# k for the later head groups: loaded as bf16 blocks by GpSimd's casting DMA and transposed by SyncE's DMA instead of by TensorE

## The chip, the core and the metric

The kernel runs on one core of one Trainium2 chip. The metric is the device time of the whole program in microseconds (us), the median of several runs.

## What is computed

Causal block attention, followed by a two-branch feed-forward layer that keeps the larger branch:

```python
# q, k, v: [8 batches, 8 heads, 576 rows, 64] float32
scores = q @ k.T / 8                       # per batch and head
scores = where(pos_i // 64 >= pos_j // 64, scores, -1e9)   # 64-row blocks
attn   = softmax(scores)
x      = (attn @ v), heads side by side    # [4608 tokens, 512]
h1, h2 = x @ w1, x @ w2                    # w1, w2: [512, 1024]
out    = maximum(h1, h2) @ w_out           # w_out: [1024, 512]
```

## The kernel before, in words

**Tiles.** Heads are handled in pairs (two heads of 64 side by side fill 128 partitions), and two pairs form a *group*: 16 groups of 4 heads, two groups to a batch. For a pair p the scores need `qT` and `kT`, bf16 tiles of 128 x 576 with the head dimension on the partitions. There are four slots of each (`kT_r[p % 4]`), so the slot that group g fills was last read by group g - 2.

**How k becomes kT.** `load_qk(g)` (L112, its DMA at L120) brings 576 KB of q and 576 KB of k of a group, as float32, through SyncE's DMA queue; each waits for a tiny GpSimd memset (L119) that holds it back to its place in the order. `cast` (L132) turns each into bf16 on GpSimd one iteration later. `transposes` (L352) does 18 transposes of 64 x 128 on TensorE into two PSUM tiles, and their contents are copied out (L360), one half by VectorE and one by ScalarE. `T_AT` says when: the even pair of group g carries the transposes of q of group g + 1, the odd pair those of k. `pad_keys` (L378) then makes on GpSimd a small zero-padded copy `kz` of the last key blocks of each pair.

**The order is written by hand.** The engines execute the instructions in the order in which the program emits them; no scheduler moves anything. The start up to group 2 is spelled out. From group 3 on, one loop over g runs (an *iteration*, one per group), with an even pair a = 2g and an odd pair b = 2g + 1:

1. `region(tile_0(a), tile_1(a))`: scores (L371), exponentials on ScalarE (L395), masks on GpSimd (L400);
2. per pair: `fill` with some units of the feed-forward part, then `av` of the pair two back (L479, its results normalised by VectorE into `xp`, L485 and L486), then the transposes of that half, then more scores; after the odd pair `pad_keys` of the next two pairs;
3. `pool_work`: GpSimd's loads of v (L136, casting DMAs of 64-element rows), the memsets that release the next loads, and the casts.

**The feed-forward part** is a list of units with a due time. `h_unit` (L215) multiplies x by w1 - w2 and `y_unit` (L257) makes a 128 x 512 piece of the output and stores it through SyncE's queue (L263). `fill(n)` runs some n matmuls of these wherever TensorE would otherwise wait. A unit may only start when the tokens that it needs are marked done (`done_tokens`).

**x by DMA.** From group 4 to 14 the attention output `xp` is turned into `xT` by two DMA transposes on SyncE's queue (`x_dma`, L497), issued after the odd pair's `av` in the iteration after the group's own. A batch is complete with its second group, so the second group's transposes must land before the first `h_unit` of that batch, which the loop starts after the first half-`fill` of the next iteration. The first `h_unit` reads the first group's two rows of `xT` (c = 0, 1), then, after six matmuls of `av`, the second group's (c = 2, 3).

**Semaphores of DMAs.** The DMAs of each kind rotate over eight semaphores, so that a DMA waits for the eighth before it on its kind of queue.

Of the kernel before, what the change touches and what calls it, by code (L numbers as in the profile page):

```python
# [9 lines left out]
BF16 = mybir.dt.bfloat16  # L10
# [4 lines left out]
def kernel(  # L15
# [10 lines left out]
    nc = tc.nc  # L26

    B, H, S, D = q.shape
    P = 128
    BLK = 64  # L30
# [14 lines left out]
    NG = NPAIR // 2  # L45
    GPB = HP // 2
# [36 lines left out]
    raw = ctx.enter_context(tc.tile_pool(name="raw", bufs=3))  # L83
# [10 lines left out]
    NV, NA, NT = 3, 4, 4  # L94
    qT_r = [ring.tile([P, S], BF16, name=f"qT{r}") for r in range(NT)]
    kz_r = [ring.tile([P, 3 * BLK], BF16, name=f"kz{r}") for r in range(NT)]
    kT_r = [ring.tile([P, S], BF16, name=f"kT{r}") for r in range(NT)]
# [12 lines left out]
    dve, pool, act = nc.vector.tensor_copy, nc.gpsimd.tensor_copy, nc.scalar.copy  # L110

    def load_qk(g, queues, gated=False):  # L112
        b, u = divmod(g, GPB)
        for nm, src, queue in (("q", q, queues[0]), ("k", k, queues[1])):
            if queue is None:
                continue
            raws[nm, g] = t = raw.tile([P, 2, RPP * D], FP32, name=f"{nm}raw")
            if gated:
                nc.gpsimd.memset(t[:, 0, :1], 0.0)  # L119
            queue.dma_start(  # L120
                out=t[:],
                in_=src[b, 4 * u:4 * u + 4].rearrange(
                    "(s h) (p t) d -> (h p) s (t d)", h=2, t=RPP),
            )

    def cast(nm, g, parts):
        t = raws[nm, g].rearrange("p s (t d) -> p t s d", d=D)
        if (nm, g) not in qk_n:
            qk_n[nm, g] = qkn.tile([P, RPP, 2, D], BF16, name=f"{nm}n")
        n = qk_n[nm, g]  # L130
        for copy, j0, j1 in parts:
            copy(out=n[:, j0:j1], in_=t[:, j0:j1])  # L132

    def load_v(b, c):
        rows = min(P, S - c * P)
        nc.gpsimd.dma_start(  # L136
            out=vv_r[b % NV][P - rows:, c, :, :D],
            in_=v[b, :, c * P:c * P + rows, :].rearrange("h p d -> p h d"),
        )
# [7 lines left out]
    for j in range(d_ff // WB):  # L147
        row, n = (1, j) if j < 3 else (3, 0)
# [22 lines left out]
    dve, pool, act = nc.vector.tensor_copy, nc.gpsimd.tensor_copy, nc.scalar.copy  # L171
# [174 lines left out]
    def transposes(nm, g, copies):  # L346
        n = qk_n.pop((nm, g))
        pts = [ps_m.tile([P, RPP, NP], BF16, name=f"ps_{nm}T", tag="m") for _ in range(2)]
        for j in range(RPP):
            for i in range(2):  # L350
                r = slice(i * NP, (i + 1) * NP)
                nc.tensor.transpose(  # L352
                    pts[i][:, j, :], n[r, j].rearrange("p s d -> p (s d)"), ident[r, r],
                )

        def copy_out(which=(0, 1), part=(0, NP), copy=None):
            p0, p1 = part
            for i in which:
                t = (qT_r if nm == "q" else kT_r)[(2 * g + i) % NT]
                (copy or copies[i])(  # L360
                    out=t[:, p0 * RPP:p1 * RPP].rearrange("q (p j) -> q p j", j=RPP),
                    in_=pts[i][:, :, p0:p1].rearrange("q j p -> q p j"),
                )
        return copy_out
# [67 lines left out]
    def tile_0(p):  # L432
        u = ps_s.tile([P, 2, 512], FP32, name="ps_s", tag="s")
        scores(p, u, 0, 0, 0, 512)
        return lambda: (exp(p, u, 512, 0), mask(p, 0))

    def tile_1(p):
        u = ps_s.tile([P, 2, 512], FP32, name="ps_s", tag="s")
        scores(p, u, 0, 0, 512, 64)
        scores(p, u, 64, 1, 128, 448)  # L440
        return lambda: (exp(p, u, 512, 512), mask(p, 576))

    def tile_2(p):
        u = ps_s.tile([P, 2, 512], FP32, name="ps_s", tag="s")
        corner_scores(p, u, 320)
        scores(p, u, 0, 2, 256, 320)
        scores(p, u, 384, 3, 448, P)

        def out():
            exp(p, u, 512, 1024)  # L450
            nc.scalar.activation(
                out=aT_r[p % NA][BLK:, :, 1536:AW], in_=u[BLK:, :, 320:320 + BLK],
                func=AF.Exp, scale=scale,
            )
            mask(p, 1024)
            mask(p, 1344)
        return out

    def region(*tiles):
        for out in tiles:  # L460
            out()
# [29 lines left out]
    def x_by_dma(g):  # L491
        return BY_DMA <= g < NG - 1

    def x_dma(g):
        b, u = divmod(g, GPB)
        for s in range(2):
            nc.sync.dma_start_transpose(  # L497
                out=xT[:, 2 * u + s, b * S:b * S + NCH * P].rearrange(
                    "p (t w) -> p t w", w=P),
                in_=xps[g][:, s].rearrange("p t a d -> p (t a d)"),  # L500
            )

    def x_out(g, t0=0, t1=NCH, copies=(dve, dve)):
        b, u = divmod(g, GPB)
        if x_by_dma(g):
            if u == GPB - 1:
                done_tokens[0] = (b + 1) * S
            return
        xp = xps[g]
        n = t1 - t0  # L510
        n_odd = min(t1, NCH - 1) - t0
        pe = ps_m.tile([P, 2, n, BLK], BF16, name="ps_xe", tag="m")
        po = ps_m.tile([P, 2, n_odd, BLK], BF16, name="ps_xo", tag="m")
        for s in range(2):
            for t in range(t0, t1):
                src = xp[:, s, t].rearrange("p a d -> p (a d)")
                nc.tensor.transpose(pe[:, s, t - t0, :], src[:BLK], ident[:BLK, :BLK])
                if t < NCH - 1:
                    nc.tensor.transpose(po[:, s, t - t0, :], src[BLK:], ident[BLK:, BLK:])
        dst = xT[:, 2 * u:2 * u + 2, b * S + t0 * P:b * S + t1 * P].rearrange(  # L520
            "p s (t h w) -> p s t h w", h=2, w=BLK)
        copies[0](out=dst[:, :, :, 0], in_=pe[:])
        copies[1](out=dst[:, :, :n_odd, 1], in_=po[:])
        if u == GPB - 1:
            done_tokens[0] = min(b * S + t1 * P, (b + 1) * S)
# [8 lines left out]
    def fill_of(g):  # L534
        if g == NG - 1:
            return 45
        left = 5 - g if g < 5 else 2 - (g - 5) % 2
        return -(-max(0, ready() - KEEP) // left)


    def pool_work(s):
        g, i = divmod(s, 2)
        if s == 4:
            load_qk(4, (SP, SP), gated=True)
        elif s == 5:
            load_qk(5, (SP, SP), gated=True)
            cast("q", 4, ((pool, 0, RPP),))
            cast("k", 4, ((pool, 0, RPP),))
        else:
            if i == 1 and g + 3 < NG:  # L550
                load_qk(g + 3, (SP, SP), gated=True)
            if i == 1 and g + 2 < NG:
                cast("q", g + 2, ((pool, 0, RPP),))
                cast("k", g + 2, ((pool, 0, RPP),))
            nb, j = divmod(s + 2, HP)
            if nb < B:
                for c in ((0, 1), (2, 3), (4,), ())[j]:
                    load_v(nb, c)

    T_AT = {s: [("qk"[s % 2], s // 2 + 1)] for s in range(NPAIR - 2)}  # L560
    T_AT[0] = T_AT[1] = T_AT[2] = T_AT[3] = []

    def t_pair(s):
        outs = [transposes(nm, g, (dve, act)) for nm, g in T_AT.get(s, [])]
        return lambda: [f() for f in outs]


# [3 lines left out]
    def av_with(p, n):  # L571
        av(p, [0, 1])
        fill(n)
        av(p, [2, 3, 4])
# [82 lines left out]
    outs = tile_0(4), tile_1(4)  # L657
# [13 lines left out]
    n = fill_of(GPB)  # L671
# [10 lines left out]
    for g in range(GPB + 1, NG):  # L682
        a, b = 2 * g, 2 * g + 1
        old = done_tokens[0]
        if x_due:
            x_out(x_due.pop())
        n, new = fill_of(g), done_tokens[0]
        region(tile_0(a), tile_1(a))
        lo, hi = max(3, n // 18), n * 2 // 9
        for p, tiles in ((a, lambda: (tile_2(a), tile_0(b))), (b, lambda: (tile_1(b), tile_2(b)))):  # L690
            if p == a and x_by_dma(g - 2):
                done_tokens[0] = old
            rest = fill(hi)
            done_tokens[0] = new
            fill(rest)
            av_with(p - LAG, lo)
            if p % 2 and x_by_dma(g - 1):
                x_dma(g - 1)
            copy_out = t_pair(p)
            outs = tiles()  # L700
            copy_out()
            region(*outs)
            if p % 2 and g + 1 < NG:
                pad_keys(p + 1)
                pad_keys(p + 2)
            pool_work(p)
        x_due.append(g - 1)
        fill(n - 2 * (lo + hi))
# [49 lines left out]
```

The softmax here doesn't subtract the row's maximum and nothing guards it: scores larger than these inputs give would overflow.

## Time and profile before

| What | Value |
|---|---|
| median of 3 runs | 259.0 us (258.83 to 259.49) |
| the profiled execution | 260.0 us, its span 258.2 us |
| instructions in the profile | 7195 |
| PE busy | 247.4 us, x2983 |
| VectorE, ScalarE, GpSimd busy | 136.1, 143.2, 110.4 us |
| TensorE clock granted | 1.00 throughout |
| one iteration of the loop, groups 5 to 13 | 13.0 us |
| DMA moved | 41.30 MB in 71265 packets |

The span is the time from the first to the last instruction of one profiled execution; 1.8 us of that execution lie around it. PE is TensorE's matmuls and PEld its weight loads, DVE is VectorE, ACT ScalarE, POOL GpSimd, SP SyncE. A matmul's recorded duration includes its way through the array, and matmuls overlap: the time that a block of them occupies is the distance between the starts of what comes before and after it.

### The profile page before, as it was taken

The page shows a single profiled execution, that of the slowest core. Times are in us where ns is not written, and L with a number is a line of the kernel's source. Part 1 is how long each engine was busy: PE and PEld are TensorE (multiplying, and loading weights), DVE is VectorE, ACT ScalarE, POOL GpSimd, SP SyncE. Part 2 cuts the span into 40 slices and gives each one's busy share as a digit, 9 for nine tenths or more (in the row PEclk, how much of TensorE's full clock was granted, in tenths as well). Part 3 has the DMA queues.
Part 4 walks back from the last instruction along what each step waited for, and adds up shares of the span by engine and source line. Part 5 has one row for each costly group of instructions (what it writes and reads, how often), then busy time and mean ns, then how long its engine had stood idle before and what let it go on. Part 6 is the DMA issues. An engine that isn't in the chain of part 4 may idle for free.

```text
span 258.2 us, 7195 instructions
## 1 busy us (share of the span) xinstructions
PE 247.4 (96%) x2983; PEld 139.1 (54%) x2983; DVE 136.1 (53%) x299; ACT 143.2 (55%) x200; POOL 110.4 (43%) x274
## 2 busy tenths in 40 slices
PE   7598899799999999999999999999999999999995
PEld 2346678646555555555555554546464655444444
DVE  4967986556584428451845184518550853443200
ACT  2798854476574857586757665766576431000111
POOL 1987950584637263726382638163813010000000
PEclk9999999999999999999999999999999999999999
DMA  6999999499569995998599949985977122202122
GB/s 244 316 206 307 217 251 246 156 102 253 129 162 257 144 188 135 245 154 225 114 244 143 186 145 224 168 196 141 91 109 110 44 56 80 83 0 81 43 104 99
DMA packets 71265, 41.30 MB, mean 160 GB/s; under 512 B 53568, under 2 KB 58048, under 8 KB 71232
## 3 DMA queue, kind: packets, MB, share of 16 engines
q1 hardware_dynamic: 28544, 31.27, 43.4%
q0 software_dynamic: 42272, 8.92, 39.9%
q10 hardware_dynamic: 416, 0.66, 0.7%
q8 instruction: 23, 0.38, 0.6%
q14 instruction: 10, 0.08, 0.1%
HBM read 34.60 MB, written 9.44 MB: 171 GB/s over the span
## 4 chain that ended last, share of the span: by engine, by line
PE 84%; DMA 8%; POOL 3%; ACT 2%; issue 1%; DVE 0%; SPq 0%; POOLq 0%; ACTq 0%
PE ps_y L257 36%; PE ps_h L215 22%; PE ps_o L479 10%; PE ps_s L371 8%; DMA qraw<-in_q_dram 5%; DMA kraw<-in_k_dram 3%; PE ps_qT L352 2%; PE ps_kT L352 2%; PE ps_w L341 1%; ACT aT L395 1%; PE ps_y L272 1%; PE ps_M L238 1%; POOL kn L132 1%; PE ps_s L389 1%; ACT qT L360 1%
## 5 line engine op out<-in xcount | busy, mean ns | idle before, releaser
L395 ACT ACTIVATE aT<-ps_s 128x1024 bf16<-128x1024 f32 (+2 forms) x100 | 95.8, 996 | 25.8 <-PE ps_s L371 24.2
L257 PE MATMUL ps_y<-wo_sb,g 128*128 128x512 bf16 x280 | 69.8, 379 | 0.0
L215 PE MATMUL ps_h<-xT,d_sb 128*128 128x512 bf16 (+3 forms) x320 | 69.2, 358 | 0.3 <-DVE d_sb L162 0.3
L220 DVE TENSOR_SCALAR g<-ps_h 128x512 bf16<-128x512 f32 (+3 forms) x80 | 50.7, 636 | 30.6 <-PE ps_h L215 28.8
L400 POOL MEMSET aT<- 64x128 bf16 x124 | 22.4, 200 | 81.8 <-ACT aT L395 81.2
L485 DVE RECIPROCAL rec<-ps_o 128x4 f32<-128x4 f32 (+1 forms) x64 | 12.1, 188 | 62.5 <-PE ps_o L479 61.7
L215 PEld LDWEIGHTS <-d_sb 128*128 128x128 bf16 x320 | 29.0, 98 | 29.1 <-issue 2.7
L479 PEld LDWEIGHTS <-aT 128*128 128x128 bf16 x960 | 37.2, 98 | 13.5 <-issue 0.8
L262 ACT COPY y<-ps_y 128x512 f32<-128x512 f32 x31 | 18.2, 587 | 44.5 <-PE ps_y L257 36.1
L257 PEld LDWEIGHTS <-g 128*128 128x128 bf16 x280 | 25.8, 98 | 29.8 <-issue 2.0
L479 PE MATMUL ps_o<-vv,aT 128*128 128x65 bf16 x960 | 39.8, 194 | 0.0
L257 PE MATMUL ps_y<-m_sb,xT 128*128 128x512 bf16 x140 | 38.2, 380 | 0.0
L136 POOL DMA_DIRECT2D vv<-in_v_dram x40 | 33.7, 848 | 1.6 <-issue 1.2
L371 PE MATMUL ps_s<-qT,kT 64*128 64x64 bf16 (+6 forms) x344 | 31.2, 280 | 1.6 <-ACT kT L360 0.7
L486 DVE TENSOR_TENSOR xp<-ps_o,rec 128x256 bf16<-128x256 f32 (+1 forms) x64 | 31.4, 491 | 2.2
L360 ACT COPY qT<-ps_qT 128x576 bf16<-128x576 bf16 (+1 forms) x17 | 10.3, 614 | 19.9 <-PE ps_qT L352 19.9
L132 POOL CAST qn<-qraw 128x1152 bf16<-128x1152 f32 (+1 forms) x16 | 16.9, 1058 | 9.1 <-DMA qraw<-in_q_dram 9.1
L257 PEld LDWEIGHTS <-xT 128*128 128x128 bf16 x140 | 12.2, 98 | 15.1 <-issue 3.5
L371 PEld LDWEIGHTS <-kT 64*128 64x128 bf16 x344 | 12.3, 94 | 11.0 <-issue 6.2
L132 POOL CAST kn<-kraw 128x1152 bf16<-128x1152 f32 (+1 forms) x15 | 17.1, 1140 | 1.4 <-DMA kraw<-in_k_dram 1.4
L360 ACT COPY kT<-ps_kT 128x576 bf16<-128x576 bf16 x15 | 9.6, 639 | 14.4 <-PE ps_kT L352 14.4
L207 POOL COPY g<-g 128x512 bf16<-128x512 bf16 x8 | 4.9, 614 | 20.7 <-DVE g L220 20.3
(58 smaller groups left out, 161.8 us busy)
## 6 DMA issues: line engine op xcount, KB each, us to landing
qraw<-in_q_dram SPq DMA_DIRECT2D x16, 576.0 KB, 5.0
out_dram<-y SPq DMA_DIRECT2D x35, 256.0 KB, 3.7
kraw<-in_k_dram SPq DMA_DIRECT2D x15, 576.0 KB, 5.8
vv<-in_v_dram POOLq DMA_DIRECT2D x32, 128.0 KB, 5.7
w1raw<-in_moe_w_dram POOLq DMA_DIRECT2D x4, 512.0 KB, 8.1
xT<-in_moe_w_dram POOLq DMA_DIRECT2D x4, 256.0 KB, 8.6
wo_sb<-in_moe_w_out_dram POOLq DMA_DIRECT2D x2, 512.0 KB, 10.0
kraw<-in_k_dram ACTq DMA_DIRECT2D x1, 576.0 KB, 5.6
```

The costliest lines, as they stand in the source:

```text
L132: copy(out=n[:, j0:j1], in_=t[:, j0:j1])
L136: nc.gpsimd.dma_start(out=vv_r[b % NV][P - rows:, c, :, :D], in_=v[b, :, c * P:c * P + rows, :].rearrange("h p d -> p h d"),)
L215: nc.tensor.matmul(pt[:, :w], d_sb[:, c, f * P:(f + 1) * P], xT[:, c, t0:t0 + w], start=(c == 0), stop=(c == NDM - 1),)
L220: nc.vector.tensor_scalar_max(g[:, f, m:m + w], pt[:, :w], 0.0)
L257: nc.tensor.matmul(py[:], lhs, rhs, start=(n == 0), stop=(n == len(terms) - 1),)
L262: (dve if i < 2 else act)(out=y[:], in_=py[:])
L360: (copy or copies[i])(out=t[:, p0 * RPP:p1 * RPP].rearrange("q (p j) -> q p j", j=RPP), in_=pts[i][:, :, p0:p1].rearrange("q j p -> q p j"),)
L371: nc.tensor.matmul(ps[:, hh, col:col + w], kT[r, k0:k0 + P], qT[r, q0:q0 + w], start=True, stop=True,)
L395: nc.scalar.activation(out=aT_r[p % NA][:, :, a0:a0 + w], in_=ps[:, :, :w], func=AF.Exp, scale=scale,)
L400: (eng or nc.gpsimd).memset(aT_r[p % NA][BLK:, :, a0:a0 + BLK], 0.0)
L479: nc.tensor.matmul(po[:, gi, hh, :], a[:, hh, a0:a0 + P], vv[:, c, h0 + 2 * hh, :], start=(mm == 0), stop=(mm == n_mm - 1),)
L486: nc.vector.tensor_mul(xp[:, :, ts[0]:ts[0] + n, p % 2].rearrange("q s t d -> q t s d"), po[:, :, :, :D], rec[:, :n].to_broadcast([P, n, 2 ...
```

## The change

From group 5 on, for k only:

- `load_qk` no longer loads k, and its memset, the cast on GpSimd, the 18 transposes on TensorE and the two copies out of PSUM are left out.
- `load_blocks` issues four casting DMAs from GpSimd's queue, one for each head of the group, in `pool_work` of the even pair of iteration g - 2, ahead of the v loads there. Each brings 9 blocks of 64 rows of 64 elements as bf16, into a tile that takes the place of the float32 one.
- `transpose_blocks` issues two DMA transposes on SyncE's queue, one per pair, after the even pair's `av` in iteration g - 1. Each reads 64 partitions x 9 x 128 elements and writes 128 partitions x 576 of `kT`.

Eleven groups (5 to 15) are concerned: 44 casting DMAs and 22 DMA transposes are added; 11 k loads, 11 memsets, 11 casts, 198 transposes on TensorE and 22 copies are removed. The rest of every engine's order is as before.

```diff
     def load_qk(g, queues, gated=False):
         b, u = divmod(g, GPB)
         for nm, src, queue in (("q", q, queues[0]), ("k", k, queues[1])):
-            if queue is None:
+            if queue is None or by_dma(nm, g):
                 continue
...
+    T_DMA = {nm: 5 for nm in "k"}
+    blk_n = {}
+
+    def by_dma(nm, g):
+        return g >= T_DMA.get(nm, NG)
+
+    def load_blocks(nm, g):
+        b, u = divmod(g, GPB)
+        blk_n[nm, g] = n = raw.tile([P, S // BLK, 2, D], BF16, name=f"{nm}b", tag=f"{nm}raw")
+        for h in range(2):
+            for s in range(2):
+                nc.gpsimd.dma_start(
+                    out=n[h * BLK:(h + 1) * BLK, :, s],
+                    in_=(q if nm == "q" else k)[b, 4 * u + 2 * s + h].rearrange(
+                        "(j p) d -> p j d", p=BLK),
+                )
+
+    def transpose_blocks(nm, g):
+        n = blk_n.pop((nm, g))
+        for h in range(2):
+            nc.sync.dma_start_transpose(
+                out=(qT_r if nm == "q" else kT_r)[(2 * g + h) % NT].rearrange(
+                    "q (j p) -> q j p", p=BLK),
+                in_=n[h * BLK:(h + 1) * BLK].rearrange("p j s d -> p (j s d)"),
+            )
+
     def cast(nm, g, parts):
+        if by_dma(nm, g):
+            return
...
             if i == 1 and g + 3 < NG:
                 load_qk(g + 3, (SP, SP), gated=True)
+            if i == 0:
+                for nm in "qk":
+                    if g + 2 < NG and by_dma(nm, g + 2):
+                        load_blocks(nm, g + 2)
...
-        outs = [transposes(nm, g, (dve, act)) for nm, g in T_AT.get(s, [])]
+        outs = [transposes(nm, g, (dve, act)) for nm, g in T_AT.get(s, []) if not by_dma(nm, g)]
         return lambda: [f() for f in outs]
...
             if p % 2 and x_by_dma(g - 1):
                 x_dma(g - 1)
+            if p % 2 == 0:
+                for nm in "qk":
+                    if g + 1 < NG and by_dma(nm, g + 1):
+                        transpose_blocks(nm, g + 1)
             copy_out = t_pair(p)
```

## The prediction

> **What bounds the kernel now.** I read the page's busy table, then its chain, then the busy time by stretches over the loop. The first column of each line of stretches is the stretch, the second its length, then each engine's busy time.
>
> ```profile
> PE 247.4 (96%) x2983; PEld 139.1 (54%) x2983; DVE 136.1 (53%) x299; ACT 143.2 (55%) x200; POOL 110.4 (43%) x274
> PE 84%; DMA 8%; POOL 3%; ACT 2%; issue 1%; DVE 0%; SPq 0%; POOLq 0%; ACTq 0%
> 112.00:125.00 13.00, 13.00 (x166) 7.09 (x164) 5.34 (x12) 9.21 (x14) 5.51 (x17) 1.00 0.71 197
> 125.00:138.00 13.00, 13.00 (x166) 7.06 (x164) 7.96 (x16) 8.15 (x12) 7.73 (x19) 1.00 1.13 173
> ```
>
> TensorE is the bound: busy in all of each 13.0 us iteration at clock 1.00, with no other engine above 9.2. The 8% of DMA in the chain lie in the first 46 us, before the first removed transpose. So in the loop only time taken from TensorE's queue, or a wait put into it, counts. A busy PE may still hide overlap, so a removed block is priced by start distances, in the timeline of TensorE (start, duration, instructions): first the odd pair of group 13, which carries k's transposes, then that of group 15, which has none.
>
> ```profile
> 177.90 0.90 PE L479 MATMUL ps_o<-vv,aT 128*128 128x65 bf16 x24
> 178.74 0.44 PE L352 MATMUL ps_kT<-ident,kn 64*128 64x64 bf16 x18
> 179.01 0.38 PE L371 MATMUL ps_s<-qT,kT 64*128 64x64 bf16 x4
> ...
> 204.49 0.90 PE L479 MATMUL ps_o<-vv,aT 128*128 128x65 bf16 x24
> 205.32 0.39 PE L371 MATMUL ps_s<-qT,kT 64*128 64x64 bf16 x4
> ```
>
> From av to scores it is 179.01 - 177.90 = 1.11 us with the block and 205.32 - 204.49 = 0.83 without: 18 transposes occupy **0.28 us**, not the 18 x 191 ns = 3.4 us of their own durations.
>
> **What the Trainium skill says.** TensorE: Matmul & The Clock Gate (Part 4: PE-mode transpose) gives about 275 ns for one transpose in a kernel, most of it latency. The trace agrees on the latency (191 ns each) and shows that it overlaps. DMA: Bandwidth & Descriptors says three things that matter. Under "Rules for kernel authors", a cast goes from GpSimd and a DMA transpose from SP or ACT, which is where the change puts them. Under "Issuing engines are not separate DMA queues", all queues share the same 16 engines and interleave; the trace agrees, x's DMA transposes land later beside v's loads (below). Under "DMA Transpose (X-bar)", a partition dimension that is a multiple of 16 is allowed; 64 is one, but this trace has only 128-partition transposes.
>
> **The change part by part.**
>
> *TensorE.* 11 blocks x 0.28 = **-3.1 us**, all on the path. From below, the blocks' busy 0.44 gives -4.8, which counts latency that overlaps; from above, the 13.0 us iterations show nothing else to win. I take -3.1.
>
> *VectorE and ScalarE* lose 11 copies of 748 and 639 ns. Nothing on the path waits for them: 0. Two PSUM tiles fewer per iteration: 0, as TensorE doesn't wait for them now.
>
> *GpSimd.* It loses 11 casts of 1154 and 11 memsets of 106 ns (13.9 us) and gets 44 issues. The nearest rows are v's issues:
>
> ```profile
> 107.00 1.75 POOL L136 DMA_DIRECT2D vv<-in_v_dram  x2
> 113.28 0.69 POOL L136 DMA_DIRECT2D vv<-in_v_dram  x1
> ```
>
> Those of 128x8 rows take 0.88, the one of 64x8 rows 0.69. A k block has 64x9 rows: 0.71 by interpolation, bounds 0.69 and 0.88, so four take 2.85 us (2.75 to 3.5), 31 us in all. GpSimd goes to some 7.1 and 9.3 of 13 us. Behind the four in its queue stand v's loads, the odd pair's masks, pad_keys, the memset that releases q and q's cast. In the fuller iteration the q cast ends at 105.98 now; with 2.85 more, less the 0.2 to 0.6 us that GpSimd idled there (0.38 before v, 0.58 and 0.71 before masks, not all recoverable), less one memset, it ends at about 107.6, and q's transposes start at 109.5. In iteration 3 the margin is smallest, about 0.5 us (cast end 56.4 + 2 against 58.96). Masks are read an iteration later. Cost 0, at worst 0.6 once.
>
> *SyncE* loses 11 k issues (0.42) and gets 22 DMA transposes. The row for x says 1.27 us of issue; k has 576 rows of 256 B where x has 640, so 1.15, or 2.3 if the price is per block (9 against 5). It is used some 6 of 13 us; the y stores behind wait for at most 2.5 to 4.6 us with four y buffers: 0. The transposes wait for blocks loaded an iteration earlier and for scores of the iteration before: no new wait. They come after the first y store of the iteration (109.33), so at about 109.8; with x's 4.0 us to land, or 7.3 at worst, they land by 114 to 118. pad_keys reads them at 117.28, the scores at 118.6. Cost 0, at worst about 0.5 in every second iteration.
>
> *DMA engines.*
>
> ```profile
> q1 hardware_dynamic: 28544, 31.27, 43.4%
> q0 software_dynamic: 42272, 8.92, 39.9%
> ```
>
> A GpSimd-queue packet costs 0.399 x 258.2 x 16 / 42272 = 39 ns. k adds 44 x 576 = 25344 packets: 62 us of each of 16 engines' time, against 23 us off for the k loads (0.434 x 258.2 us x 6.5 of 31.3 MB). The share of the stretches above goes from 0.7 to 1.1 to above 1 (queues overlap, so it isn't capped at 1). What is late next? **x's transposes.** They are issued after the odd pair's av, and four times (iterations 6, 8, 10, 12) they complete a batch while the k blocks, issued 1.4 us earlier, flow. Now:
>
> ```profile
> L497 SPq DMA_TRANSPOSE xT<-xp x2: 1206/1218/1230, 114.7 to 116.0; - x2
> DMA to landing us min/median/max: 2.9/3.2/3.5
> ...
> 121.04 0.81 PE L215 MATMUL ps_h<-xT,d_sb 128*128 128x512 bf16 x3
> ...
> L497 SPq DMA_TRANSPOSE xT<-xp x2: 1211/1284/1357, 153.7 to 154.9; - x2
> DMA to landing us min/median/max: 4.7/5.2/5.7
> ```
>
> The first pair is such an iteration, with one small v load beside it: the first lands 3.5 us after its issue (I take the longer time for the first, which then lands just before the second). h reads those rows at 121.04, after the change 0.28 earlier: 121.04 - 0.28 - 114.67 = 6.1 us of budget. The second pair is an iteration with two v loads (2048 rows, issued just as far ahead): the first needs 5.7 us; others like it 5.0, 5.5 and 6.9. With four k blocks and a small v, 2816 rows, I add 0.7 us (768 rows at about 1100 a us, the rate at which 2 x 1024 rows land): 5.7, 6.2, 6.4, 7.6. Against 6.1 that is a stall of 0 to 1.5 us, 1.9 over four places; bounds 0 (GpSimd issues k slower than v, 576 per 0.71 us, so x keeps its turn) and 6.
>
> *v behind k.* The third part of v is now issued at 113.28 + 2.85 and is read at the end of the next even av, about 6 us later; beside x, v loads took 3.5 to 7.3 us to land. It falls in the same iterations, and a stall on x gives it the same time: 0 more, at worst 1.3 where x is on time.
>
> **Sum.** -3.1 + 1.4 (between no stall and 1.9, nearer the latter) = **-1.7 us**. Against the profiled execution (260.0: span 258.2 and 1.8 around) that is 258.3; it lies 1.0 above the median, 259.0, so the median becomes **257.3**.
>
> **The rivals.**
> 1. *All hidden*: k's slower issue leaves x its turn. For it: after the first half microsecond x's transposes are limited by SyncE's 1.2 us of issue each. -3.1: 255.9.
> 2. *x late decides* (ends slower): every second iteration TensorE stands at the third matmul of the batch's first h_unit. Price: landing less 6.1 us, four times. It breaks even at 0.78 us a place, a landing at 6.9, which the trace has once among four (179.7). At 7.5 to 8 us, with 64-partition transposes of k costing more than x's and lying ahead in the same queue, it is 4 x 1.4 to 1.9 = +6 to +8, less 3.1: about 262. Against: three of four disturbed landings are at 5.7 or less.
> 3. *Nothing is won*: the change leaves a wait in TensorE's queue (on kT or v) that just eats the 3.1: 259.0. Against it stands the margin of 2 us or more at the scores. That the blocks cost nothing on TensorE is excluded by 1.11 against 0.83.
>
> **How the numbers follow.** 0.3% of 259.0 is 0.8 us, about what a measurement of this kernel can tell from no change. Partly hidden (257.3, own range 256.4 to 258.5): 0.43. All hidden (255.4 to 256.4): 0.22. x late (259.8 to 263): 0.23. Nothing won (258.5 to 259.8): 0.12. Faster, below 258.2: 0.22 and most of 0.43, 0.59; same 0.18; slower 0.23. Half of the late case lies below 261.5 and a tenth of the hidden one below 255.4, so 255.4 to 261.5 leaves out less than 2 in 10; signs differ, so the likeliest case's own range stands above.
>
> **What would show it.** Right: 198 matmuls fewer on PE; kT's scores without idle time before them; TensorE's only new wait is L215's (renumbered) on x's landing, at four places 26 us apart, under 1 us each; iterations of about 12.7 us, 13 or so where x is late. k issues near 0.71, SyncE's kT transposes near 1.15 us. Wrong: landings of x above 7 us; TensorE waiting for kT or v; q's transposes waiting for GpSimd's cast; block removal worth 0.44 or under 0.2 us.

## The result, and the profile after

The changed kernel takes **267.4 us** in the median of 4 runs (265.0 to 270.9), the kernel before 259.1 us: a ratio of **1.029, 95% interval 1.022 to 1.036**. It is slower, and lies outside the forecast range. Medians are of all executions; ratios and intervals, here and below, leave out those over 1.5% above the fastest one of the same kernel. The profiled execution is the quickest of the four, 265.0 us with a span of 263.1 us, 4.9 us more than the span before. What follows explains that execution.

The page of the changed kernel gives the busy time and the chain of waits that ended last.

```profile
PE 246.1 (94%) x2785; PEld 136.4 (52%) x2785; DVE 129.1 (49%) x288; ACT 137.2 (52%) x189; POOL 130.3 (50%) x296
...
PE 69%; DMA 18%; POOL 4%; ACT 3%; SPq 2%; DVE 1%; issue 1%; ACTq 0%; POOLq 0%
PE ps_y L285 25%; PE ps_h L243 20%; DMA xT<-xp 10%; PE ps_o L507 9%; PE ps_s L399 6%; PE ps_w L369 3%; DMA kraw<-in_k_dram 3%; DMA vv<-in_v_dram 3%; DMA qraw<-in_q_dram 2%; SPq L525 2%; PE ps_qT L380 2%; ACT aT L423 2%; POOL kb L137 1%; PE ps_y L300 1%; PE ps_M L266 1%
```

TensorE has its 198 matmuls fewer, but its share of the chain falls from 84% to 69% and DMA's rises from 8% to 18%. More than half of that is one transfer, x's DMA transpose, which was not in the chain before. The waits of TensorE (who waited for whom: us in total, times, longest) give the price:

```profile
PE ps_h L243 <- DMA xT<-xp: 5.5, 5, 1.9
PE ps_o L507 <- DMA vv<-in_v_dram: 2.5, 1, 2.5
```

These are 8.0 us of new idle time. Less the 3.1 us that the removed transposes were forecast to free it is +4.9, the difference of the spans, but that agreement is chance. The two profiled executions also differ at the start, where TensorE waits for the first cast of q (before, then after):

```profile
PE ps_qT L352 <- POOL qn L132: 1.6, 1, 1.6
PE ps_qT L380 <- POOL qn L160: 0.4, 1, 0.4
```

The matmuls behind this wait start at 47.38 us before and at 46.07 after, 1.3 us earlier. This is scatter: experiment 3, with the same start as the kernel before, has no such wait. Matched one by one from there on, TensorE's matmuls win 0.27 us at each of the eleven removed blocks, 3.0 us in all, and lose 9.1 us at the waits: 2.7 on v and 6.4 on x. (The recorded waits are about 0.2 us shorter each, because a matmul's recorded end lies behind the start of the next one.) So the loop is 6.1 us longer, and the spans differ by 4.9 only because of the start.

TensorE's timeline shows one of the four places where x is late (two of the five waits lie at one place), and the answer for x's tile shows the transposes that it waited for.

```profile
95.61 0.38 PE L243 MATMUL ps_h<-xT,d_sb 128*128 128x512 bf16 x1
97.38 0.59 PE L243 MATMUL ps_h<-xT,d_sb 128*128 128x512 bf16 x2 [1.39 <-DMA xT<-xp]
...
L525 SPq DMA_TRANSPOSE xT<-xp x2: 1218/1270/1322, 89.5 to 90.8; - x2
DMA to landing us min/median/max: 5.7/6.1/6.6
```

The first matmul at 95.61 reads the first transpose's rows and isn't held; the next one starts at 97.38. The chain has x's transfer from 90.77 for 6.56 us, so it is the *second* transpose of the pair, with the longer time, that lands at 97.33; the first had landed at 95.16. The four places cost 1.4, 1.9, 1.1 and 1.1 us. The v wait is in the chain too:

```profile
61.42 2.90 POOL kb L137 x4
64.32 6.98 DMA vv<-in_v_dram
71.34 0.34 PE ps_o L507 x6
```

v's third part is issued behind the four k blocks, at 64.32, and lands 7.0 us later. It stands alone, because the batch of that iteration gets its x from TensorE and no stall on x gives v time. The queues' packets answer to those of before:

```profile
q0 software_dynamic: 68320, 12.16, 61.9%
q1 hardware_dynamic: 38928, 28.03, 47.4%
```

GpSimd's queue carries 26048 packets more (25344 by count of rows). Each costs 0.619 x 263.1 x 16 / 68320 = 38 ns, against 39 before.

### The profile page after: what moved, and what is told of

The parts are those of the page before. It is cut to its first block, busy times and chain, and to the rows that moved or that the text cites. A ratio compares the mean times of both kernels' runs of the same rounds, so it can differ in the third digit from the quotient of the medians.

```text
span 263.1 us, 6840 instructions
## 1 busy us (share of the span) xinstructions
PE 246.1 (94%) x2785; PEld 136.4 (52%) x2785; DVE 129.1 (49%) x288; ACT 137.2 (52%) x189; POOL 130.3 (50%) x296
## 3 DMA queue, kind: packets, MB, share of 16 engines
q0 software_dynamic: 68320, 12.16, 61.9%
## 4 chain that ended last, share of the span: by engine, by line
PE 69%; DMA 18%; POOL 4%; ACT 3%; SPq 2%; DVE 1%; issue 1%; ACTq 0%; POOLq 0%
PE ps_y L285 25%; PE ps_h L243 20%; DMA xT<-xp 10%; PE ps_o L507 9%; PE ps_s L399 6%; PE ps_w L369 3%; DMA kraw<-in_k_dram 3%; DMA vv<-in_v_dram 3%; DMA qraw<-in_q_dram 2%; SPq L525 2%; PE ps_qT L380 2%; ACT aT L423 2%; POOL kb L137 1%; PE ps_y L300 1%; PE ps_M L266 1%
## 5 line engine op out<-in xcount | busy, mean ns | idle before, releaser
L164 POOL DMA_DIRECT2D vv<-in_v_dram x40 | 34.4, 872 | 0.0
L137 POOL DMA_DIRECT2D kb<-in_k_dram x44 | 32.3, 751 | 1.0 <-issue 0.5
L388 DVE COPY qT<-ps_qT 128x576 bf16<-128x576 bf16 (+1 forms) x17 | 12.1, 712 | 0.4 <-PE ps_qT L380 0.2
## 6 DMA issues: line engine op xcount, KB each, us to landing
out_dram<-y SPq DMA_DIRECT2D x35, 256.0 KB, 4.1
xT<-in_moe_w_dram POOLq DMA_DIRECT2D x4, 256.0 KB, 8.5
```

Source lines behind the costliest of these rows:

```text
L137: nc.gpsimd.dma_start(out=n[h * BLK:(h + 1) * BLK, :, s], in_=(q if nm == "q" else k)[b, 4 * u + 2 * s + h].rearrange("(j p) d -> p j d", ...
L164: nc.gpsimd.dma_start(out=vv_r[b % NV][P - rows:, c, :, :D], in_=v[b, :, c * P:c * P + rows, :].rearrange("h p d -> p h d"),)
L388: (copy or copies[i])(out=t[:, p0 * RPP:p1 * RPP].rearrange("q (p j) -> q p j", j=RPP), in_=pts[i][:, :, p0:p1].rearrange("q j p -> q p j"),)
```

## The experiments

**Theory A**: the k rows on GpSimd's queue share the DMA engines with x's transposes and v's third part just when TensorE is about to need those. **Theory B**: k's own DMA transposes, ahead of x's in SyncE's queue, delay x.

**1. The transposes alone** (`e4_dma_transpose_only`).

```diff
-            if queue is None or by_dma(nm, g):        # load_qk: k comes as before
+            if queue is None:
-        if by_dma(nm, g):                              # cast: on GpSimd as before
-            return
-        n = blk_n.pop((nm, g))                         # transpose_blocks
+        n = qk_n.pop((nm, g))
-                        load_blocks(nm, g + 2)
```

> The other half alone: k comes as float32 through SyncE and is cast by GpSimd as before, and SyncE's DMA transposes it instead of TensorE. The keys of a pair come out in another order than the masks and v expect, which changes values and not the work. Theory A: no k rows on GpSimd's queue, so the gain of 3.1 us is there with little lost, 256.0 to 257.0 us. Theory B: x's four stalls are there, 261 to 263 us.

Measured: 255.5 us, ratio 0.987 (0.984 to 0.990), half a microsecond better than A's range. TensorE waits for no DMA in the loop; x's transposes land as before the change, with k's own 22 in the same queue:

```profile
L523 SPq DMA_TRANSPOSE xT<-xp x2: 1207/1240/1272, 111.9 to 113.2; - x2
DMA to landing us min/median/max: 2.7/3.0/3.3
```

Theory B falls as a cause by itself. This half of the change alone is a gain.

**2. The loads alone** (`e3_blocks_tensore`).

```diff
-                        transpose_blocks(nm, g + 1)
...
-        outs = [transposes(nm, g, (dve, act)) for nm, g in T_AT.get(s, []) if not by_dma(nm, g)]
+        outs = [transposes(nm, g, (dve, act)) for nm, g in T_AT.get(s, [])]
...
+        blocks = by_dma(nm, g)
+        n = (blk_n if blocks else qk_n).pop((nm, g))
...
+                    in_=pts[i].rearrange("q j p -> q (j p)") if blocks else
```

> Half of the change alone: k's blocks are loaded by GpSimd's casting DMAs as in the changed kernel, but TensorE transposes them and VectorE and ScalarE copy them out, as before. Theory A (loads): all stalls of the changed kernel stay and its gain is gone, 259.1 + 8 = 267 us (265 to 270). Theory B (k's DMA transposes ahead of x's): x lands on time, only v's wait of 2.5 us is left, about 261.5 us.

Measured: 264.9 us, ratio 1.021 (1.016 to 1.025). The stalls on x are there without any DMA transpose of k:

```profile
PE ps_h L243 <- DMA xT<-xp: 3.8, 4, 1.5
```

This is nearer to A, a little below its 265, but not all stalls stay. x's are 3.8 instead of 5.5 us, and the 2.5 us wait on v is gone: v's third part, issued at 64.27 us behind the same four k blocks, lands in 3.6 us instead of 7.0. In the changed kernel two DMA transposes of k, issued at 56.8 and 58.4 us, were then still under way, until 64.7 and 66.0. So the loads are enough to make x late; k's transposes beside them make the loss larger, and of these kernels v is late only in the one that has both. The two halves' changes, +6.1 and -3.3 us, add up to +2.8, the whole change to +8.3.

**3. The freed TensorE time alone** (`e5_no_k_transposes`).

```diff
-        outs = [transposes(nm, g, (dve, act)) for nm, g in T_AT.get(s, [])]
+        outs = [transposes(nm, g, (dve, act)) for nm, g in T_AT.get(s, []) if nm == "q" or g < 5]
```

> The kernel before without the 198 transposes of k for groups 5 to 15 and their 22 copies out of PSUM; loads and casts stay. kT is not refreshed, so the scores use old keys. It prices the freed TensorE time alone. If the start distances in the trace are right (0.28 us a group): 259.1 - 3.1 = 256.0 us (255.6 to 256.4). If the block's recorded 0.44 us is what it occupies: 254.3. If the time was slack: 259.1.

Measured: 256.5 us, ratio 0.990 (0.988 to 0.993), just above the first range. The same line two iterations apart, in TensorE's timeline, gives the block's price without the start's scatter:

```profile
82.88 0.59 PE L257 MATMUL ps_y<-m_sb,xT 128*128 128x512 bf16 x2 [0.16 <-issue]
...
108.35 0.60 PE L257 MATMUL ps_y<-m_sb,xT 128*128 128x512 bf16 x2 [0.16 <-issue]
```

Two iterations take 25.47 us instead of 26.0, so a block occupies 0.27 us, 2.9 us over eleven. The 0.44 us of its recorded duration would have given 25.1.

**4. v ahead of k** (`e1_v_first`): in `pool_work` of the even pair, `load_blocks` after the v loads.

```diff
-            if i == 0:
-                for nm in "qk":
-                    if g + 2 < NG and by_dma(nm, g + 2):
-                        load_blocks(nm, g + 2)
...
                     load_v(nb, c)
+            if i == 0:
+                for nm in "qk":
+                    if g + 2 < NG and by_dma(nm, g + 2):
+                        load_blocks(nm, g + 2)
```

> The changed kernel with one order turned round: in the even half GpSimd issues v's part ahead of the four k blocks. Theory A: v's wait of 2.5 us, which stands at one place where x isn't late, goes, and the four stalls on x stay, since the same rows flow during x's transposes: 2 to 3 us less than the changed kernel, 262 to 265 us. If v behind k were what holds everything (a stall on x that only follows from it), 256 to 258 us.

Measured: 261.9 us, ratio 1.010 (1.007 to 1.014), just under A's range. The profiled executions are 2.5 us apart, the medians 5.5.

```profile
PE ps_h L243 <- DMA xT<-xp: 4.8, 5, 1.3
```

The wait on v is gone and the stalls on x stay. v is late only when it is issued behind the k blocks; x is late in either order.

**5. The k blocks half an iteration later** (`e2_k_odd_half`): out of x's way, one group further ahead.

```diff
-                    if g + 2 < NG and by_dma(nm, g + 2):      # i == 0
-                        load_blocks(nm, g + 2)
+            for n in (g + 2, g + 3) if g == GPB + 1 else (g + 3,):     # after v
+                if i == (n == g + 3) and n < NG and by_dma("k", n):
+                    load_blocks("k", n)
```

> The four k block loads of a group move by half an iteration: they are issued after the odd pair's v loads, an iteration further ahead (group g + 3), so that they flow when x's transposes have landed; everything else is as in the changed kernel. Theory A (the k rows on GpSimd's queue share the DMA engines with x's transposes and v's third part just when TensorE is about to need those): all stalls go and the 3.1 us of the removed transposes remain, 256.0 us (255.5 to 257.0). Theory B (k's own DMA transposes, ahead of x's in SyncE's queue, delay x): x's four stalls of about 1.5 us stay, only v's wait of 2.5 us goes, 261 to 263 us.

Measured: 259.0 us (257.0 to 262.8), ratio 0.999 (0.997 to 1.001): a miss for A's number. Its timeline has no wait on x at all, but two new ones just after iteration 3, into which the edit had put the blocks of two groups:

```profile
65.23 0.61 PE L399 MATMUL ps_s<-qT,kT 64*128 64x512 bf16 x6 [0.39 <-DMA kT<-kb]
70.34 0.34 PE L507 MATMUL ps_o<-vv,aT 128*128 128x65 bf16 x6 [1.29 <-DMA vv<-in_v_dram]
```

**6. The same from group 6 on** (`e9_k_odd_half_from6`), without the pile; the diff is against experiment 5:

```diff
-    T_DMA = {nm: 5 for nm in "k"}
+    T_DMA = {nm: 6 for nm in "k"}
```

> The k blocks issued in the odd half, an iteration further ahead, as before, but from group 6 on, so that iteration 3 no longer issues the blocks of two groups. Theory A (what the first such kernel still lost were v's and kT's waits of 1.3 and 0.4 us just after iteration 3, from my piling of eight issues there): ten groups' gain, 258.8 - 2.8 = 256.0 us (255.6 to 256.8). Rival (k's rows on GpSimd's queue cost wherever they are put): 258 to 259 us with stalls spread over the loop.

Measured: 257.0 us (256.0 to 258.5), ratio 0.994 (0.991 to 0.997). It leaves nothing of the computation out, and is 0.6% faster than the kernel before. No wait on x, v or kT is left in the loop, and two iterations take 25.47 us, as in experiment 3. It stays 1 us above A's number; its profiled execution waits 1.6 us for the first casts of q at 47 us, as the kernel before did.

**7. Half and twice the rows** (`e10_half_rows`, `e11_double_rows`). The k blocks that stay in the even half stand behind v, as in experiment 4.

```diff
+            if i == 1 and g + 3 < NG and by_dma("k", g + 3):      # half: from group 6 on
+                load_blocks("k", g + 3, (0,))
+            if i == 0 and g + 2 < NG and by_dma("k", g + 2):
+                load_blocks("k", g + 2, (1,))
...
+        for dst in (n, spare):                                    # twice, from group 5 on
```

> Half the dose: from group 6 on two of a group's four k blocks are issued in the odd half, as in the kernel that moved all of them, and two (1152 rows) stay in the even half, behind v, where x's transposes run. Theory A with x's landing growing with the rows beside it (second transpose: about 3.3 us with none, 6.4 with 2304): about 4.9 us, just inside what TensorE allows, so 256 to 257.5 us. Rival (any k rows there make x wait for its turn, however many): stalls as with all four, 260 to 262 us.

> Twice the dose: as the kernel that issues v ahead of k in the even half, with every k block loaded a second time into a tile that nobody reads (4608 rows beside x's transposes, 5.9 us of issue). Theory A: x's second landing goes from about 6.4 to 9 or more us, four stalls of some 3 to 4 us: 258.9 - 3.1 + 14 = 270 us (265 to 278, GpSimd's own lateness on q's cast included). Rival (x only waits for its turn once): 262 to 263 us.

Half measured 257.2 us, ratio 0.993 (0.991 to 0.995), with one stall on x of 0.5 us. Twice measured 285.7 us, ratio 1.103 (1.094 to 1.112), more than A's range: x costs 10.2 us, and a second wait joins it.

```profile
PE ps_qT L382 <- POOL qn L162: 11.8, 7, 3.1
PE ps_h L245 <- DMA xT<-xp: 10.2, 7, 2.0
...
100.67 1.46 POOL L139 DMA_DIRECT2D spare<-in_k_dram  x2 [1.88 <-DMA vv<-in_v_dram]
```

GpSimd had to wait between its issues for a DMA to land (last line, its timeline), its q cast came late, and TensorE's transposes of q waited. So twice the rows is no clean dose for x; it only shows that GpSimd then falls behind as well.

The table gives, for the four iterations that complete a batch, the time from the issue of x's first transpose until both have landed, as read from the profiles for each transpose by itself, and TensorE's wait on x there. "k rows beside x" are those issued in the same half of the iteration.

| kernel | k rows beside x | both landed, us after the first issue | wait on x, us |
|---|---|---|---|
| before | 0 | 5.3, 4.8, 4.8, 3.9 | none |
| transposes alone | 0 | 3.9, 3.9, 4.9, 3.9 | none |
| odd half, from group 6 | 0 | 3.9, 5.7, 4.3, 3.9 | none |
| half | 1152 | 5.8, 7.2, 5.7, 5.7 | 0, 0.5, 0, 0 |
| loads alone | 2304 | 8.4, 7.0, 8.8, 6.6 | 1.5, 0.3, 1.9, 0 |
| v ahead of k | 2304 | 7.2, 7.0, 8.9, 7.7 | 0.8, 0.6, 2.3, 1.3 |
| after | 2304 | 7.8, 8.4, 7.7, 7.6 | 1.4, 1.9, 1.1, 1.1 |

The landing grows with the rows beside it. TensorE waits wherever it takes more than about 6.5 us (6.7 to 6.9 with the loads alone, where TensorE still transposes k).

**8. The short rows on SyncE's queue** (`e6_sync_blocks`, and `e8_sync_blocks_qk` for q as well).

```diff
+            if by_dma(nm, g):
+                raws[nm, g] = t = raw.tile([P, RPP, 2, D], FP32, ...)
+                ...
+                        queue.dma_start(
+                            out=t[h * BLK:(h + 1) * BLK, :, s],
+                            in_=src[b, 4 * u + 2 * s + h].rearrange("(j p) d -> p j d", p=BLK))
```

> k as float32 in 64-row blocks through SyncE's queue (four DMAs of 576 rows of 256 B in place of one with 256 rows of 2304 B), cast by GpSimd as before, and transposed by SyncE's DMA: the keys keep their order, and all results are the reference's. Theory A: these rows are released after x's transposes and lie behind them in the same queue, so no stall on x: 255.5 to 256.5 us, faster than both kernels. Rival (it is the number of short rows, on whatever queue, that starves the rest): stalls on x, v or kT, 258 us or more.

> The same for q and k from group 5 on: 22 blocks of transposes leave TensorE. If the DMA engines and SyncE's queue take it (six transposes of 1.25 us and eight more loads an iteration), 258.8 - 6.2 = 252.6 us. If not, q's transposes, which are wanted half an iteration earlier than k's, or the y stores behind them in SyncE's queue come late: 254 to 262 us.

k alone: 265.9 us in the median of ten runs (259.9 to 268.1), ratio 1.006 (1.002 to 1.010). q and k: 300.1 us, ratio 1.158 (1.155 to 1.161). In both A's number is missed, and in both profiles it is kT that comes late. TensorE's largest wait, of k alone (the longest run, 268.1 us) and then of both:

```profile
PE ps_s L407 <- DMA kT<-kn: 9.5, 5, 2.3
...
PE ps_s L407 <- DMA kT<-kn: 31.3, 10, 4.6
```

The rival's forecast held: with k as 2304 rows of 64 elements instead of 256 rows of 2304 bytes, even the quickest run, 259.9 us, is 4.4 us above experiment 1 with its long rows. Whether the rows on the engines or SyncE's three more issues a group make kT late was not separated, and no profile shows one of the quicker runs.

## Why the prediction was wrong

The direction was wrong. Rival 2, "x late decides", given 0.23, is what happened. Its price for x, 6 to 8 us, fits the 6.4 that x cost in the profile, though k's transposes ahead in the queue, its reason, are not enough by themselves (experiment 1); the total of about 262 left out v's wait and what the longer runs added.

- **TensorE's gain** held: 0.28 us a block was forecast, 0.27 measured by iteration length.
- **x's landing is the step that failed.** The prediction put x's stalls at 1.9 us over four places and took 1.4; the profile has 5.5. It priced the pair's first transpose only and let the second land right behind it, because it took the longer of the two times for the first. In the quiet pair that it shows, the first needs 2.9 us and the second 3.5, so the second lands 1.9 us after the first; in the other pair the first does have the longer time. After the change the first transposes landed no later than forecast: in 5.3, 5.7, 6.1 and 7.1 us, sorted, where the prediction had 5.7, 6.2, 6.4 and 7.6. But, place by place, the second landed 2.2, 2.3, 0.6 and 2.2 us after the first, and it is the one that TensorE waits for most: at the first place 97.33 - 89.50 = 7.8 us from the first issue, where TensorE was free for it at 95.99, after 6.5. So the 0.7 us for the extra rows was enough for the first transpose, and the second had no term at all. "GpSimd issues k slower than v, so x keeps its turn" was no protection: GpSimd was still issuing k, until 91.0 us, when x's second transpose was issued at 90.77. Why the second falls back that far was not separated.
- **v behind k** was put at 0, "the same iterations, and a stall on x gives it the same time". In iteration 4 nothing gave it time: batch 1's x comes from TensorE. Its budget there was not 6 us but 68.8 - 64.3 = 4.5; it took 7.0. This is the 2.5 us. Experiment 2 adds that this landing needed k's DMA transposes beside the loads; the prediction priced neither effect on v.
- **Sum**: by TensorE's timeline -3.0 + 6.4 + 2.7 = +6.1 us in the loop of the profiled execution, against -1.7 forecast. Its span grew by 4.9, since its start was 1.3 us quicker.
- **GpSimd** held: a k issue takes 751 ns on average (0.71 forecast, 0.69 to 0.88), q's cast was never late in the changed kernel's loop. **SyncE** held too: 1.2 to 1.4 us for 15 of k's 22 transposes, up to 2.35, where 1.15 was forecast; the scores waited for kT nowhere.
- **The Trainium skill's rule** that all queues run on the same 16 engines and interleave (DMA: Bandwidth & Descriptors, "Issuing engines are not separate DMA queues") was cited, and its price taken too low. The table above agrees with it, but no run shows in which part of the shared path x's transposes lose their time.

Open: the other three runs of the changed kernel were 2 to 6 us longer than the profiled one. They have no profile, so what they waited for isn't shown; a part of it is likely the clock (last section). That the two halves' changes don't add up is measured; which of k's transposes meets which rows was not taken apart further.

## What to carry to other kernels

When work moves from the bounding engine to DMA, list the transfers that the engine waits for next and compare each one's landing, beside the new traffic, with the time at which it is read; a transfer with a microsecond to spare is the next bound. Of transfers issued as a pair, price the one that lands last. Count rows, not bytes: here k as 2304 rows of 64 elements a group made x late from GpSimd's queue and went with a late kT on SyncE's, and as 256 long rows with the same DMA transpose it gave the whole gain. If the short rows are needed, move them in time: issued half an iteration later they cost nothing that the loop shows.

## What the runs showed of the hardware that was not expected

- TensorE's granted clock can fall after stalls. In the trace of experiment 2, TensorE waits 0.4 and 1.5 us for x within 2.3 us, and its clock then reads 0.50 from 151 to 154 us: the stretch from the matmul at 150.45 to that at 154.27 takes 3.8 us, where the changed kernel takes 2.1 (151.84 to 153.92) at clock 1.00. That is 1.7 us beyond the wait. Experiment 4's trace shows the same after waits of 1.1 and 1.2 us (0.50 from 149 to 152). It doesn't follow each stall: the changed kernel's profiled execution has a mean clock of 1.000 with waits of 2.5 and 1.9 us.
- The means of experiments 2 and 4 are 0.994 and 0.993. The three longer runs of the changed kernel have 0.994, 0.987 and 0.981; (1 - clock) times the span gives an estimate of 1.6, 3.4 and 5.1 us lost by it, where these runs took 2.9, 2.1 and 6.0 us more than the profiled one. So the clock can be much of the difference, but no profile confirms it. Two runs of the kernel before also read 0.993, at 262.0 and 262.8 us.
- k's DMA transpose from 64 partitions, which the trace before didn't have, costs SyncE about the same as x's from 128: mostly 1.2 to 1.4 us of issue each, and 3.4 to 7.9 us to land.
